# Router logits of the dilated heads: class-ordered read from SBUF, stepped write to PSUM

## The chip, the cores and the metric

The kernel runs on one core of one Trainium2 chip. The metric is the device time of one execution in microseconds; several executions are taken and their median is given. The profile that is read below is of one such execution, taken by the hardware profiler.

A core has TensorE (PE), which multiplies matrices, VectorE (DVE), ScalarE (ACT) and GpSimd (POOL) for everything else, and SyncE (SP), which issues most of the transfers. Data lies in SBUF, in 128 partitions. TensorE reads its two operands from SBUF and writes to PSUM, from where DVE or ACT fetch the result.

## The reference

Two blocks follow each other. The first is windowed attention over a batch of 8, with 8 heads, 576 positions and 64 features a head. The first four heads are plain: a position sees the 32 positions up to itself. The last four are dilated by 4: a position sees every fourth of the last 128. The second block is a mixture of 8 experts over the 4608 tokens with 512 features each (8 heads x 64):

```python
logits = np.einsum('bsd,de->bse', x, w_gate)
local_gate = 1.0 / (1.0 + np.exp(-np.einsum('bsd,de->bse', x, w_local).squeeze(-1)))
...
        fresh_e = int(np.argmax(logits[b, s]))
        if s == 0 or local_gate[b, s] < 0.5:
            e = fresh_e
        else:
            e = prev_e if prev_e >= 0 else fresh_e
...
        h = np.maximum(x[b, s] @ w1[e], 0.0)
        out[b, s] = p[e] * (h @ w2[e])
```

So each token has 8 logits and one locality value, and goes either to the expert with the largest logit or to the expert of the token before it. Everything is in float32. The change concerns the first two lines, the matrix product of the features with `w_gate` and `w_local`.

## The kernel before

**Stages.** The attention stage runs until some 158 us; then the experts' stage runs to the end. A second, exact version of the whole is in the program and runs only if a value leaves its bounds (`again > 0`, line 208); it does not run here.

**Order of a dilated head.** On the host, q, k and v of the dilated heads are put in the order of their class, that is of the position modulo 4 (`_by_class`, line 1231): first the 144 positions 0, 4, 8, ..., then 1, 5, 9, ..., and so on (`DIL` = 4, `CI` = 144, `S` = 576). In this order dilated attention is plain attention within a class. Its output stays in this order: in the tile `xt`, which holds the features of one pair of batches (`GB` = 2, `GS` = 1152 tokens) with features on the partitions, `xt[:, 0]` has the plain heads in natural order and `xt[:, 1]` the dilated heads in class order. Each has two chunks of 128 features (`CH` = 2), so there are `DK` = 4 chunks `kk` in all.

**Attention loop (line 1091).** Step `n` handles two heads of one batch. TensorE computes `scores(n)` (masks at L322 in bf16, scores at L329 in f32), ACT takes the exponential, and `values(n - 1)` multiplies with the values (L381), using `vt`, whose shifted part GpSimd copies (`share`, L270). Every second step `turn` transposes the finished heads into `xt` (L402, L406, copied by ACT at L403 and L408) and `store` writes them to DRAM. SyncE loads keys and values three steps ahead (L261, L266) into buffers that `values` frees.

**Routing.** When four pairs of heads of a pair of batches have been turned, `route` puts the routing steps of that pair into a list, `waiting`, and `gap` takes a few of them between the matmuls of the attention loop, by hand-written costs. The first step is `logits`, the next are `fresh` (transposes at L445), `carry` and so on, up to the lists of tokens of each expert. For the last pair of batches `logits` is called at once, at the end of the attention stage; its remaining steps run beside the first experts. Routing decides which rows GpSimd gathers (L847) and which weights SyncE loads (L773).

**`logits` (line 420).** `lp` is one PSUM bank of 128 partitions x 288 columns. The 1152 tokens are cut into `NC` = 4 runs of `NQ` = 288 tokens; run `c` goes to the 32 partitions from `c * LW`, each with its own column tile of the array (`tile_position=(0, c * LW)`), and the 9 used weight columns (padded to 32) are the stationary operand. For each chunk `kk` the four runs follow each other, and the four chunks accumulate in PSUM. For the plain heads (`kk` < 2) the moving operand is 288 neighbouring floats of each partition. For the dilated heads it has to be brought into natural order: element `4 j + c` is read from `xt[..., c * 144 + j]`. ACT then copies `lp` to `le` (L437), and `fresh` transposes `le`.

Of the kernel before, what the change touches and what calls it, by code (L numbers as in the profile page):

```python
# [23 lines left out]
B, H, S, DH = 8, 8, 576, 64  # L24
# [4 lines left out]
WIN, DIL = 32, 4  # L29
# [19 lines left out]
CH = 2  # L49
# [7 lines left out]
NQ = GS // NC  # L57
LW = 32
# [154 lines left out]
def whole(ctx, tc, exact, bad, qk, v, wgl, w1, w2, con, adm, msk, qmk, out, cst, wg, ones):  # L213
    nc = tc.nc
# [31 lines left out]
    def bank(shape, name):  # L246
        return banks.tile(shape, F32, name=name, tag="bank")
# [172 lines left out]
    def logits(g):  # L420

        st = routes[g]
        xt = st["xt"]
        lp = bank([P, NQ], "lp")
        for kk in range(DK):
            for c in range(NC):
                if kk < CH:
                    rhs = xt[:, 0, kk, c * NQ:(c + 1) * NQ]
                else:
                    b, s = divmod(c * NQ, S)  # L430
                    rhs = xt[:, 1, kk - CH, b * S:(b + 1) * S].rearrange("p (c j) -> p j c", c=DIL)
                    rhs = rhs[:, s // DIL:(s + NQ) // DIL]
                nc.tensor.matmul(lp[c * LW:(c + 1) * LW], lhsT=wg[:, kk], rhs=rhs,
                                 start=(kk == 0), stop=(kk == DK - 1), skip_group_check=True,
                                 tile_position=(0, c * LW))
        st["le"] = le = sm.tile([P, NQ], F32, name="le")
        nc.scalar.copy(le, lp)  # L437
# [613 lines left out]
    def route(g, slow):  # L1051
        steps = [(logits, 0, True), (fresh, 3.0, True), (carry, 1.0, True), (carry_over, 0.5, True), (carry_in, 0.5, True),
                 (choose, 1.5, True), (gate, 1.5, False), (place, 0.5, True), (lanes_of, 1.3, False)]
        if slow:
            logits(g)
            steps.pop(0)
        for f, *how in steps:
            waiting.append((lambda f=f: f(g), *how))
            if slow and f == fresh:
                waiting.append(pause)  # L1060
        waiting.extend((f, cost, False) for f, cost in zip(matrices(g), (0.9, 0.9, 0.9, 1.7)))
        if g in (EARLY - 1, NG - 1):
            late = g == NG - 1
            counts = count(late)
            steps = [(lambda: next(counts), 1.8, True)] * (PASSES + 1 if exact and late else 2)
            waiting.append(steps.pop())
            waiting.append((lambda: products(g, False), 0.3, True))
            waiting.extend(steps)
            waiting.append(pause)
            waiting.append((lambda: table(late), 0.3, True))  # L1070
            if late:
                waiting.append((late_tokens, 1.5, True))
            else:
                waiting.append((early_tokens, 1.5, True))
                waiting.append((early_weights, 0, False))
        else:
            waiting.append(pause)
            waiting.append((lambda: products(g, not g), 0.3, True))
# [200 lines left out]
```

## Time and profile before

| | |
|---|---|
| time, median of 3 runs | 675.02 us (674.6 to 676.7) |
| the profiled execution, whole | 672.8 us |
| its span, first to last instruction | 670.9 us |
| `logits` matmuls, L433 | 128 records, mean 544 ns |
| copy of `lp` by ACT, L437 | 4 of 398 ns |
| DMA moved | 126.38 MB, mean 188 GB/s |

A page of the profile gives the busy time of each engine, the span in forty equal slices (a digit is the busy share in tenths), and groups of equal instructions: line, engine, operation, output and inputs with their shape, count, then the time that the group covers, the mean of one in nanoseconds, and the idle time of the engine before it with what ended it. Other views list the instructions in order of time, the waits by who was waited for, or stretches of time with each engine's busy time (in brackets the number of instructions), TensorE's granted clock as a share of full speed, the share of time that the 16 DMA engines were busy, and GB/s. Records that run at the same time on different parts of TensorE's array count once in a group's covered time and each in full in its mean. An f32 matmul appears as two records.

### The profile page before, as it was taken

The numbers are of one execution on the slowest core, as the hardware profiler recorded it, in microseconds if no ns is written. First come the engines' busy times: TensorE is split into PE (matmuls) and PEld (weight loads), VectorE is DVE, ScalarE is ACT, GpSimd is POOL, SyncE is SP. The second block draws the span as 40 slices with busy tenths as digits, with TensorE's granted clock in tenths as the row PEclk, the third lists the DMA queues.
The fourth block names the chain that finished last, engine by engine and source line by source line (L and its number), as shares of the span: only waits on it lengthen the run. The fifth ranks groups of instructions, "written<-read, shape, count | busy, mean of one in ns | idle before, by whom it ended". The sixth has DMA issues, their size and how long they took to land. (4 is left out here: it accounts for less than half of the span.)

```text
span 670.9 us, 15284 instructions
## 1 busy us (share of the span) xinstructions
PE 655.1 (98%) x6466; PEld 572.1 (85%) x6466; DVE 373.7 (56%) x755; ACT 188.7 (28%) x348; POOL 186.6 (28%) x162
## 2 busy tenths in 40 slices
PE   8999999999999999999999999999999999999996
PEld 6988888787769999999589989997889988899893
DVE  3548669474397587363455581727373637446441
ACT  3544343432112232322223213222222232213210
POOL 3322212132023420321560343414044213041011
PEclk9999999999999999999999999999999999999999
DMA  8989889746403289666452545741054452353001
GB/s 325 321 274 310 279 263 324 244 138 240 196 33 146 91 355 386 228 221 214 140 233 75 219 173 185 288 143 60 9 189 166 182 218 98 123 221 145 1 33 49
DMA packets 29357, 126.38 MB, mean 188 GB/s; under 512 B 4221, under 2 KB 13789, under 8 KB 25312
## 3 DMA queue, kind: packets, MB, share of 16 engines
q1 hardware_dynamic: 22480, 106.10, 43.7%
q0 software_dynamic: 6800, 19.21, 8.3%
q8 instruction: 53, 0.87, 0.5%
q14 instruction: 24, 0.20, 0.1%
HBM read 142.07 MB, written 19.20 MB: 240 GB/s over the span
## 5 line engine op out<-in xcount | busy, mean ns | idle before, releaser
L971 POOL DMA_INDIRECT out_dram<-y,tok x36 | 55.0, 1528 | 297.0 <-DVE y L1040 124.0
L943 PE MATMUL hp<-xc,sum 128*128 128x128 f32 x720 | 85.6, 276 | 0.4 <-DVE sum L810 0.4
L943 PEld LDWEIGHTS hp<-xc,sum 128*128 128x128 f32 x720 | 82.8, 192 | 0.8 <-PE hp L943 0.5
L1025 PE MATMUL yp<-sum,hc 128*128 128x256 f32 x360 | 82.7, 380 | 0.0
L953 DVE TENSOR_TENSOR h<-hp,h 128x512 f32<-128x512 f32 x45 | 30.9, 690 | 90.4 <-PE hp L943 89.7
L1025 PEld LDWEIGHTS yp<-sum,hc 128*128 128x128 f32 x360 | 68.3, 190 | 9.6 <-ACT y L1033 0.4
L1040 DVE SCALAR_TENSOR_TENSOR y<-yp,gate,y 128x256 f32<-128x256 f32 x45 | 21.7, 482 | 75.3 <-issue 48.1
L270 POOL COPY vt<-vt 32x1040 f32<-32x1040 f32 x32 | 34.5, 1081 | 95.8 <-DMA vt<-in_v_dram 67.8
L943 PE MATMUL hp<-xe,raw 128*128 128x128 f32 x480 | 58.8, 276 | 0.0
L943 PEld LDWEIGHTS hp<-xe,raw 128*128 128x128 f32 x480 | 56.6, 192 | 1.8 <-issue 1.5
L1025 PE MATMUL yp<-raw,h 128*128 128x256 f32 x240 | 57.0, 381 | 0.0
L847 POOL DMA_INDIRECT xg<-xd,tok x40 | 46.0, 1149 | 38.1 <-PE hp L943 15.3
L329 PE MATMUL two<-kq 64*96 64x64 f32 x1152 | 54.9, 245 | 0.0
L329 PEld LDWEIGHTS two<-kq 64*96 64x96 f32 x1152 | 52.8, 162 | 0.0
L1025 PEld LDWEIGHTS yp<-raw,h 128*128 128x128 f32 x240 | 44.5, 190 | 5.5
L947 ACT COPY h<-hp 128x512 f32<-128x512 f32 x45 | 26.3, 585 | 79.3 <-PE hp L943 75.4
L334 DVE SCALAR_TENSOR_TENSOR pr<-two,mk 96x512 f32<-96x512 f32 x32 | 21.9, 684 | 47.9 <-ACT pr L336 37.7
L381 PE MATMUL pv<-vt,pr 96*64 96x65 f32 x1280 | 46.1, 226 | 2.1 <-POOL vt L270 1.6
L847 POOL DMA_INDIRECT xg<-xd,pos x40 | 44.2, 1104 | 12.1 <-issue 10.7
L954 ACT ACTIVATE h<-h 128x512 f32<-128x512 f32 x45 | 28.3, 630 | 67.2 <-DVE h L953 67.2
L381 PEld LDWEIGHTS pv<-vt,pr 96*64 96x64 f32 x1280 | 41.0, 139 | 5.1 <-POOL vt L270 1.9
L1033 ACT ACTIVATE y<-yp,gate 128x256 f32<-128x256 f32 x45 | 21.2, 473 | 56.1 <-PE yp L1025 50.0
(222 smaller groups left out, 1013.4 us busy)
## 6 DMA issues: line engine op xcount, KB each, us to landing
raw<-in_w_dram SPq DMA_DIRECT2D x48, 2048.0 KB
kq<-in_qk_dram SPq DMA_DIRECT2D x32, 592.0 KB
vt<-in_v_dram SPq DMA_DIRECT2D x32, 292.5 KB
xd<-x SPq DMA_DIRECT2D x16, 512.0 KB
raw<-in_w_dram SPq DMA_DIRECT2D x4, 512.0 KB
xd<-x SPq DMA_DIRECT2D x16, 64.0 KB
xg<-xd,tok POOLq DMA_INDIRECT x40, 3.2
xg<-xd,pos POOLq DMA_INDIRECT x40, 3.3
```

Source lines behind the costliest of these rows:

```text
L270: nc.gpsimd.tensor_copy(vt[:WIN, :, 1:], vt[QB:, :, :NB - 1])
L329: nc.tensor.matmul(sc[:KW, u, (i - a) * QB:(i - a + 1) * QB], lhsT=kt[h, i * QB:i * QB + KW], rhs=qt[h, i * QB:(i + 1) * QB], start=bool(a ...
L334: nc.vector.scalar_tensor_tensor(pr, sc[:KW, :, :w], -CEIL, mk[:, kind].unsqueeze(1).to_broadcast([KW, 2, w]), Alu.max, Alu.min)
L381: nc.tensor.matmul(pv[h * QB:(h + 1) * QB, k - a, u], lhsT=p[:, u, (i - c) * QB:(i - c + 1) * QB], rhs=vt[:, u, i], start=True, stop=True, ...
L847: nc.gpsimd.indirect_dma_start(out=x[:rows, g], out_offset=None, in_=xd[g] if units[u]["late"] else xd[g][:EARLY * GS], in_offset=bass.Ind ...
L943: nc.tensor.matmul(to[:, m], lhsT=a[:, m, kk], rhs=b[:, kk], start=first and m == 0 and kk == 0, stop=(kk == DK // 2 - 1), skip_group_chec ...
L947: nc.scalar.copy(at((0, 1, 3)[k]), of)
L953: nc.vector.tensor_tensor(at(k), of, at(k), op=Alu.add)
L954: nc.scalar.activation(at(k), at(k), Act.Relu)
L971: nc.gpsimd.indirect_dma_start(out=out, out_offset=bass.IndirectOffsetOnAxis(ap=of_unit(u, "tok", j), axis=0), in_=y, in_offset=None, boun ...
L1025: nc.tensor.matmul(to, lhsT=a[:, m], rhs=b[:, m], start=first and m == 0, stop=(m == FK // 2 - 1), skip_group_check=True)
L1040: nc.vector.scalar_tensor_tensor(at(k), of, of_unit(u, "gate", k // 2), at(k), Alu.mult, Alu.add)
```

## The change

Only the moving operand and the output of the dilated heads' matmuls in `logits` are described differently. Before, the operand was read in natural order: the inner index went over the 4 classes, 144 floats apart, the outer over 72 positions `j` one float apart. The output was 288 neighbouring columns. Now the inner index of the operand goes over 72 neighbouring positions, and the outer over the 4 classes. The output is given the same order: for each class 72 columns that are four columns (16 bytes) apart in PSUM. Each product still reaches the same column of `lp`. The plain heads' matmuls, the weights, the accumulation flags and the number of matmuls are as before.

```diff
             for c in range(NC):
+                to = lp[c * LW:(c + 1) * LW]
                 if kk < CH:
                     rhs = xt[:, 0, kk, c * NQ:(c + 1) * NQ]
                 else:
                     b, s = divmod(c * NQ, S)
-                    rhs = xt[:, 1, kk - CH, b * S:(b + 1) * S].rearrange("p (c j) -> p j c", c=DIL)
-                    rhs = rhs[:, s // DIL:(s + NQ) // DIL]
-                nc.tensor.matmul(lp[c * LW:(c + 1) * LW], lhsT=wg[:, kk], rhs=rhs,
+                    rhs = xt[:, 1, kk - CH, b * S:(b + 1) * S].rearrange("p (c j) -> p c j", c=DIL)
+                    rhs = rhs[:, :, s // DIL:(s + NQ) // DIL]
+                    to = to.rearrange("p (j c) -> p c j", c=DIL)
+                nc.tensor.matmul(to, lhsT=wg[:, kk], rhs=rhs,
                                  start=(kk == 0), stop=(kk == DK - 1), skip_group_check=True,
                                  tile_position=(0, c * LW))
```

## The prediction

> **What bounds the kernel now.** I read the page's busy times first, then its forty slices, then the groups of instructions kept apart by shape, then the timeline and the stretches around the touched matmuls, and last what TensorE waited for.
>
> ```profile
> PE 655.1 (98%) x6466; PEld 572.1 (85%) x6466; DVE 373.7 (56%) x755; ACT 188.7 (28%) x348; POOL 186.6 (28%) x162
> ...
> PE   8999999999999999999999999999999999999996
> ...
> L433 PE MATMUL lp<-xt,wg 128*32 128x288 f32 x128 | 12.7, 544 | 0.0
> ...
> L437 ACT COPY le<-lp 128x288 f32<-128x288 f32 x4 | 1.6, 398 | 10.5 <-PE lp L433 10.5
> ```
>
> TensorE is busy 655.1 of 670.9 us, in every slice, and no other engine passes 56%. So time taken from TensorE should come off the end, unless a stage is held by something else. The change touches one group, L433: 128 records that together cover 12.7 us. Four of them run beside each other, since each writes its own 32 rows of `lp`; hence 544 ns each and 12.7 us for all. There are four calls of `logits`, one per pair of batches, each with 4 chunks `kk` x 4 column tiles `c` x 2 records (the trace shows an f32 matmul as two records) = 32 records, that is 8 passes of four.
>
> The timeline around the first call, TensorE alone (start, us, engine, line, operation, count):
>
> ```profile
> 41.97 0.34 PE L406 MATMUL tp<-cst,x 64*128 64x64 f32 x2
> 42.24 3.20 PE L433 MATMUL lp<-xt,wg 128*32 128x288 f32 x32
> 45.36 0.41 PE L322 MATMUL two<-am 64*96 64x320 bf16 x6
> ```
>
> From the first start to the start of the next line 3.12 us pass. Asked in narrow windows, the same line gives the starts of the passes:
>
> ```profile
> L433 PE MATMUL lp<-xt,wg x4: 406/406/406, 42.7 to 42.8; 128*32 128x288 f32 x4
> ...
> L433 PE MATMUL lp<-xt,wg x4: 676/686/690, 44.2 to 44.2; 128*32 128x288 f32 x4
> ```
>
> Passes begin at 42.24, 42.49, 42.74, 42.99, then 43.24, 43.70, 44.22 and 44.74. The first four (kk 0 and 1, the plain heads, read as 288 neighbours) take 0.25 us each. The last four (kk 2 and 3, the dilated heads, each element 144 floats from the one before) take 0.46, 0.52, 0.52 and 0.62 us, the last with the drain until the next line starts; a record grows from 406 to some 680 ns. As two stretches:
>
> ```profile
> 42.24:43.24 1.00, 1.00 (x18) 0.55 (x21) 1.00 0.84 335
> 43.24:45.36 2.12, 2.12 (x20) 0.44 (x12) 1.00 0.81 235
> ```
>
> The granted clock is 1.00 in both, so the doubling is the access pattern's, not the throttle's. The other calls agree: 81.45 to 84.58, 129.14 to 132.26 and 157.82 to 160.92, thus 3.13, 3.12 and 3.10 us.
>
> Does anything else set the pace around these calls? The DMA engines are nearly full before 112 us (0.98 to 1.03 of their time in some 4 us stretches), so a faster TensorE could meet late loads. Its list of waits has the largest of that kind as
>
> ```profile
> PE hp L943 <- DVE h L953: 1.7, 2, 0.9
> PE pv L381 <- POOL vt L270: 1.6, 2, 1.2
> ```
>
> 1.6 us for the shifted value tile, both times in 136 to 160 us, and the score matmuls of L329 never waited for their keys. GpSimd waited 67.8 us for value loads at L270, but that reached TensorE only there: in the tightest place I looked at, the copy that starts at 63.85 ends at 64.89 and its reader starts at 67.77, 2.9 us later.
>
> [...]
>
> **The change, part by part.**
>
> *Removed:* the strided read in 4 of 8 passes of each call. The new read is four runs of 72 neighbours, three jumps in 288 elements. At the price of kk 0 and 1 those passes would take 4 x 0.25 = 1.00 us, plus the drain at the end of the call, which I take from the last pass: 0.62 - 0.50 = 0.12 us. So 2.12 becomes 1.12: 1.00 us saved a call, 4.0 us in all, if the write costs nothing.
>
> *Added:* PSUM writes 16 bytes apart in the same passes[...]. There is no row for it; I bound it. From below: nothing, a pass stays at 0.25 us. (Less than the contiguous pass is excluded, as the matmul and its operands are the same.) From the trace's fastest contiguous write, the bf16 mask matmuls of L322: two of them, on different rows of the array and into different banks, pass in the 0.18 us before the next line:
>
> ```profile
> 53.86 0.34 PE L322 MATMUL two<-am 64*96 64x320 bf16 x2
> 54.04 1.66 PE L329 MATMUL two<-kq 64*96 64x64 f32 x36
> ```
>
> 320 columns in 0.18 us is 0.56 ns a column[...]. The f32 pass delivers a column only every 0.25 us / 288 = 0.87 ns. [...] So f32, being slow itself, hides most or all of what would hurt bf16. From above: [...] I estimate four contiguous passes, 1.00 us. I take 0.25[...].
>
> *Unchanged:* 16 matmuls a call, their weights, flags and waits, no DMA, no queue moved. Each value lands in the same column of `lp`, so L437 (398 ns) and the transposes at L445 see the same layout. L437 starts earlier by what the call saves; its 10.5 us of waiting is ScalarE's and is in nobody's way.
>
> *Where the saving goes.* After calls one to three, scores of the next heads follow directly on TensorE (45.36, 84.58, 132.26), and after the fourth L917, the first expert. Loads are issued by SyncE when TensorE frees a buffer, so they move with it; the gathers hang on the routing that moves too. From 172 us on TensorE has no wait over 1 us, so the end moves with it. What could be late next is the value tile, with 2.9 us of slack at the tightest place seen, where 1.0 us has been gained; I charge nothing, and up to 1.0 us for the range. One more thing can move: from 149.2 to 152.6 us the granted clock is halved, after a stretch with only 1.98 us of TensorE work in 3.2:
>
> ```profile
> 146.00:149.20 3.20, 1.98 (x50) 1.77 (x48) 2.65 (x11) 1.33 (x2) 1.55 (x2) 1.00 0.58 193
> 149.20:152.60 3.40, 3.40 (x33) 2.83 (x27) 1.43 (x5) 0.92 (x2) 1.51 (x2) 0.50 0.14 39
> ```
>
> In it 8 transposes of L402 took 1.97 us against 1.09 elsewhere. Shifted work may meet this differently, by about 1 us either way.
>
> *Sum:* span 670.9 - 4.0 = 666.9; the profiled execution took 672.8, so it would take 668.8. The median of the runs shown is 675.02, 2.2 above that execution (674.6 to 676.7), so the forecast against it is 675.0 - 4.0 = 671.0 us.
>
> **The rivals.**
> - *Absorbed.* Passes drop to 0.25 us but late loads take most of it back before 160 us, where the loads end. Only the fourth call's 1.0 us is left for certain: 674.0. For it: DMA shares near 1.0. Against: no wait of L329, and slack in the value tiles. Chance 0.05.
> - *Trade of one stride for the other.* [...] 0.50 to 0.65 us. Four passes then take 2.0 to 2.6 us, plus 0.12, against 2.12: 0.0 to +0.6 us a call, 675.0 to 677.4. For it: the strided read shows that a fetch of one f32 alone does double a pass, although f32 is slow already; the f32 rate hid nothing there. [...] Chance 0.15, a fifth of it beyond 677.
> - *The write is worse than the read (the slower side).* Place: kk 2 and 3 of `logits`, in PSUM. [...] 1.00 us a pass: 4.12 against 2.12, +2.0 us a call, +8.0 in all, 683.0. It decides from 0.50 us a pass upward, and is measurable from 0.63 (2 us / 16 passes above 0.50). [...] Chance 0.32.
>
> **How the numbers follow.** The forecast, passes at 0.25 to 0.32 us, has 0.48. It spans 671.0 - 1.4 (an earlier end by the clock) to 671.0 + 4 x 4 x 0.07 + 0.7 = 672.8, so 669.6 to 672.8 for itself. A measurement of this kernel tells about 0.3% from no change, 2.0 us. Faster by more: the forecast, 0.48. Within: absorbed 0.05 and four fifths of the trade 0.12, so 0.17. Slower: 0.32 + 0.03 = 0.35. The range runs from 669.6 to 683.5 and leaves out some 0.05 below, and the costlier third of the last rival above, 0.11.
>
> **What would show it.** In the changed profile the group at L433 should have a mean near 410 ns instead of 544 and cover some 8.8 us instead of 12.7; a call should last about 2.1 us from its first start to the next line's. If kk 2 and 3 keep records of some 680 ns the trade is right; at 1,000 ns or more the slower rival. If L433 shrinks and the span doesn't, new waits at L381 or L329 for loads would show the absorption. The prediction is wrong if a pass with the stepped write takes more than 0.4 us.

## The result and the profile after

| | before | changed |
|---|---|---|
| time, median of 22 runs each | 676.66 us (674.6 to 681.13) | 673.79 us (669.37 to 679.94) |
| ratio to the kernel before | | 0.9948, 95% interval 0.9928 to 0.9967 |
| the profiled execution, whole | 672.8 us | 670.79 us |
| its span | 670.9 us | 668.9 us |

The ratio, which leaves out one slow run of the changed kernel, is 3.5 us less (2.2 to 4.9 us, taken of 676.66), where the two medians differ by 2.9. 4.0 us less was forecast. In the changed kernel the `logits` matmul stands at line 435 and the copy at 439. From the page's busy times, and from the groups kept apart by shape:

```profile
PE 649.8 (97%) x6466; PEld 571.0 (85%) x6466; DVE 373.1 (56%) x755; ACT 188.7 (28%) x348; POOL 185.3 (28%) x162
...
L435 PE MATMUL lp<-xt,wg 128*32 128x288 f32 x128 | 8.6, 409 | 0.1
L435 PEld LDWEIGHTS lp<-xt,wg 128*32 128x32 f32 x128 | 3.9, 109 | 3.0 <-PE tp L406 0.2
L439 ACT COPY le<-lp 128x288 f32<-128x288 f32 x4 | 1.6, 398 | 6.4 <-PE lp L435 6.4
```

The group covers 8.6 us in place of 12.7, and one record takes 409 ns in place of 544. ScalarE's copy is as long as before and waits 4.1 us less for it. The timeline of TensorE around the first call, and the same call cut at the fourth pass into two stretches:

```profile
42.35 2.15 PE L435 MATMUL lp<-xt,wg 128*32 128x288 f32 x32
44.43 0.41 PE L322 MATMUL two<-am 64*96 64x320 bf16 x6
```

```profile
42.35:43.35 1.00, 1.00 (x17) 0.55 (x21) 1.00 0.95 331
43.35:44.43 1.08, 1.08 (x20) 0.39 (x12) 1.00 0.97 355
```

The second half, which writes PSUM four columns apart, now takes 1.08 us, of which the drain is part; it took 2.12. A pass late in that half looks like the early ones:

```profile
L435 PE MATMUL lp<-xt,wg x4: 406/406/406, 44.1 to 44.1; 128*32 128x288 f32 x4
```

406 ns: the stepped write adds nothing to an f32 pass. All four calls last 2.08 us, so they give back 1.04, 1.05, 1.04 and 1.02 us, 4.15 together. The first expert's matmul, before and then changed:

```profile
160.92 2.43 PE L917 MATMUL hp<-xe,raw 128*128 128x256 f32 x10
```

```profile
156.73 3.72 PE L919 MATMUL hp<-xe,raw 128*128 128x256 f32 x16
```

It starts 4.19 us earlier, yet the span is only 2.0 us shorter: 2.2 us are lost again in the experts' stage, which the change doesn't touch. TensorE's longest waits in the changed kernel:

```profile
PE pv L381 <- POOL vt L270: 2.1, 4, 0.8
PE cold L283 <- DVE before L300: 1.9, 1, 1.9
PE hp L945 <- DVE h L955: 1.7, 2, 0.9
PE tp L406 <- DVE rec L385: 1.7, 2, 0.9
PE yp L987 <- issue: 1.5, 2, 1.1
PE hp L945 <- DVE sum L812: 1.0, 1, 1.0
```

Of these, longer than before are, in the attention stage, L381 by 0.5 us and L406 by 0.9; in the experts' stage L987, a stop of 1.5 us for which the profile shows no releaser, and L945's wait for DVE's weight sums, by 0.6 us. That the attention stage nevertheless gave the whole 4.15 us is in part accident: in the profile of before it holds the spell of half clock from 149.2 to 152.6 us (0.50), in that of the changed kernel none (1.00 in each stretch from 142 to 160 us).

So three questions were left: why the write costs nothing, whether all of the 4.15 us reaches the end, and whether the 2.2 us in the experts' stage is a price of the change.

### The profile page after: what moved, and what is told of

It is laid out like the page before. It is cut to its first block, busy times and chain, and to the rows that moved or that the text cites. A ratio compares the mean times of both kernels' runs of the same rounds, so it can differ in the third digit from the quotient of the medians.

```text
span 668.9 us, 15284 instructions
## 1 busy us (share of the span) xinstructions
PE 649.8 (97%) x6466; PEld 571.0 (85%) x6466; DVE 373.1 (56%) x755; ACT 188.7 (28%) x348; POOL 185.3 (28%) x162
## 5 line engine op out<-in xcount | busy, mean ns | idle before, releaser
L945 PE MATMUL hp<-xc,sum 128*128 128x128 f32 x720 | 85.7, 275 | 1.0 <-DVE sum L812 1.0
L945 PEld LDWEIGHTS hp<-xc,sum 128*128 128x128 f32 x720 | 82.9, 192 | 1.4 <-PE hp L945 1.1
L945 PE MATMUL hp<-xe,raw 128*128 128x128 f32 x480 | 58.8, 276 | 0.0
L945 PEld LDWEIGHTS hp<-xe,raw 128*128 128x128 f32 x480 | 56.6, 192 | 1.8 <-issue 1.5
L381 PE MATMUL pv<-vt,pr 96*64 96x65 f32 x1280 | 45.9, 224 | 2.3 <-POOL vt L270 2.1
L381 PEld LDWEIGHTS pv<-vt,pr 96*64 96x64 f32 x1280 | 40.8, 137 | 5.3 <-POOL vt L270 2.6
```

What stands on the lines that cost most here:

```text
L381: nc.tensor.matmul(pv[h * QB:(h + 1) * QB, k - a, u], lhsT=p[:, u, (i - c) * QB:(i - c + 1) * QB], rhs=vt[:, u, i], start=True, stop=True, ...
L945: nc.tensor.matmul(to[:, m], lhsT=a[:, m, kk], rhs=b[:, kk], start=first and m == 0 and kk == 0, stop=(kk == DK // 2 - 1), skip_group_chec ...
```

## The experiments

**A stepped write at bf16's rate.** The first question has two answers: the step is free, or f32 is too slow to show its cost. The bf16 mask matmuls can tell. The identity that they read has its columns permuted on the host, so the read stays in one run and the result is the same.

```diff
-    m = np.concatenate([np.eye(QB)] + [np.where(m, 0.0, MASK) for m in m], 1)
+    eye = np.eye(QB).reshape(QB, QB // 4, 4).transpose(0, 2, 1).reshape(QB, QB)
+    m = np.concatenate([eye] + [np.where(m, 0.0, MASK) for m in m], 1)
...
-                        nc.tensor.matmul(sc[:KW, u, rows[0] * QB:rows[1] * QB],
+                        to = sc[:KW, u, rows[0] * QB:rows[1] * QB]
+                        nc.tensor.matmul(to.rearrange("p (i j c) -> p i c j", j=QB // 4, c=4),
...
-                                         rhs=am[h, :QB].unsqueeze(1).to_broadcast([QB, rows[1] - rows[0], QB]),
+                                         rhs=am[h, :QB].rearrange("p (c j) -> p c j", c=4).unsqueeze(1).to_broadcast([QB, rows[1] - rows[0], 4, QB // 4]),
```

> The changed kernel, and besides it the bf16 mask matmuls (320 columns, two rows of tiles at once, 0.18 us a pair) write four columns apart in PSUM too, with the identity's columns permuted so that the result and the read stay the same. Theory A, the slow f32 rate hides the step: [...] a pair grows from 0.18 us to about 0.30 to 0.36 us and the attention stage by 32 x 0.12 to 0.18 = 4 to 6 us. Theory B, a step of four columns in PSUM costs a matmul nothing at any of these rates: a pair stays at 0.18 us and the time is the changed kernel's.

The group of the larger mask matmuls in the changed kernel, where they still write neighbouring columns; then the groups of this kernel, and one pair in its timeline:

```profile
L322 PE MATMUL two<-am 64*96 64x320 bf16 x64 | 11.4, 329 | 0.8 <-DVE pr L334 0.8
```

```profile
L324 PE MATMUL two<-am 64*96 64x320 bf16 x64 | 15.6, 463 | 0.8 <-DVE pr L336 0.8
...
L324 PE MATMUL two<-am 64*96 64x64 bf16 x64 | 5.3, 250 | 0.0
```

```profile
54.62 0.47 PE L324 MATMUL two<-am 64*96 64x320 bf16 x2
54.89 1.71 PE L331 MATMUL two<-kq 64*96 64x64 f32 x36
```

The group covers 15.6 us where it covered 11.4, and a pair takes 0.27 us from its start to the next line, where it took 0.18. So the step costs bf16 half as much again: 0.27 us / 320 = 0.84 ns for a lone column, against 0.56 for one of a contiguous run. Theory A holds in kind, a little below its lower figure (0.30 us). The small masks (64 columns), which add to what is in PSUM where the larger ones overwrite, pay too: 250 ns for one in place of 198. An f32 pass brings a column only every 0.87 ns (0.25 us / 288), so it can hide the step, but nothing is left over. In the trace's own start times the stepped f32 passes follow each other every 0.242 us (43.347, 43.589, 43.832 and 44.074), 0.84 ns a column, and the bf16 pair takes 0.27 us, also 0.84 ns: the two paces can't be told apart. One reservation stays: the masks run as two matmuls on different rows of the array into two banks, `logits` as four on different columns into one. That the pace alone makes the difference between bf16 and f32 fits both, but a bf16 matmul in the place of the f32 one wasn't run. The time of this kernel, 672.12 us in its one run beside 672.27 for the kernel before, tells little beside a scatter of several us; the rows above carry the reading.

**Other distances.** The same edit with steps of 2 and of 16 columns.

> The changed kernel, with the bf16 mask matmuls writing two columns (8 bytes) apart instead of four. The run with four columns showed a pair at 0.27 us against 0.18. [...]

> The changed kernel, with the bf16 mask matmuls writing sixteen columns (64 bytes) apart. If the cost is one access for each lone column, however far apart: 0.27 us a pair, as with four columns. If it grows with the distance: more than 0.30 us.

With a step of two columns, then with sixteen:

```profile
L324 PE MATMUL two<-am 64*96 64x320 bf16 x64 | 15.8, 469 | 0.8 <-DVE pr L336 0.8
```

```profile
L324 PE MATMUL two<-am 64*96 64x320 bf16 x64 | 15.6, 463 | 0.8 <-DVE pr L336 0.8
```

15.8 and 15.6 us: the cost comes in full at a step of 8 bytes and doesn't grow to 64. Pairs of neighbouring columns with gaps between the pairs weren't run, so what a pair costs isn't shown. The one time of each of these runs, 682.06 and 682.38 us, lies 10 us above that of the run with four columns, and 5 above the median of the kernel before beside them (677.39). The mask rows are alike and don't explain that. In both profiles TensorE waits 2.9 us for `xe` from ScalarE; the mean granted clock is 0.992 and 0.997.

**The same question for the read.** Before, the elements lay 576 bytes apart. Here the plain heads too are read with a step (and written with the same one, so that the result stays), of 16 bytes and of 8.

```diff
                 if kk < CH:
-                    rhs = xt[:, 0, kk, c * NQ:(c + 1) * NQ]
+                    rhs = xt[:, 0, kk, c * NQ:(c + 1) * NQ].rearrange("p (j c) -> p c j", c=4)
+                    to = to.rearrange("p (j c) -> p c j", c=4)
```

(`c=2` for the step of 8 bytes.)

> The changed kernel, and besides it the plain heads are read four floats (16 bytes) apart and written four columns apart; the result is the same. Theory A, [...] the four passes of kk 0 and 1 take 0.52 us instead of 0.25 and a call 2.08 + 1.08 = 3.2 us. Theory B, the doubling before came from the long hop of 576 bytes: passes stay at 0.25 to 0.3 us and a call at 2.1 us. If read step and write step added up, a pass would be longer than 0.52 us.

> The changed kernel, and besides it the plain heads are read two floats (8 bytes) apart and written two columns apart; the result is the same. [...] passes stay at 0.25 us and a call at 2.1 us. If any step on the read costs: passes of kk 0 and 1 between 0.3 and 0.5 us, a call at 2.3 to 3.1 us.

A pass of kk 0 (first) and one of kk 2 (second) with the 16-byte read, from narrow windows, then the timeline of the first call with the 16-byte and with the 8-byte read:

```profile
L436 PE MATMUL lp<-xt,wg x4: 688/690/692, 43.8 to 43.8; 128*32 128x288 f32 x4
...
L436 PE MATMUL lp<-xt,wg x4: 423/423/424, 45.3 to 45.3; 128*32 128x288 f32 x4
```

```profile
43.27 3.20 PE L436 MATMUL lp<-xt,wg 128*32 128x288 f32 x32
46.40 0.41 PE L322 MATMUL two<-am 64*96 64x320 bf16 x6
```

```profile
43.27 2.19 PE L436 MATMUL lp<-xt,wg 128*32 128x288 f32 x32
45.39 0.41 PE L322 MATMUL two<-am 64*96 64x320 bf16 x6
```

With 16 bytes a record takes 690 ns and a call 3.13 us, as long as the kernel before; with 8 bytes a call takes 2.12 us, 0.04 more than in the changed kernel. So a step of 16 bytes doubles a pass just as one of 576 does (0.52 us in place of 0.25), and one of 8 bytes doesn't: the long hop isn't what the read was charged for. The 16-byte run has both steps in kk 0 and 1, and its passes (43.3, 43.8, 44.3, 44.8, 45.3) are no longer than those with the read step alone. So the write step is free beside the slow read too. Whether two costs would add isn't tested by that, since an f32 pass pays nothing for the write step by itself.

**Does a saved us reach the end?** Both kernels with every call's matmuls done three times over, which makes three times the difference.

```diff
-        for kk in range(DK):
+        for kk in [*range(DK)] * 3:
```

> The kernel before, with the 16 matmuls of each logits call done three times over in the same bank (the first matmul of each turn overwrites; the result is the last turn's). Theory A, every us of these matmuls is a us of the end: 4 calls x 2 turns more x 3.0 us = +24 us against before, about 700 us. Theory B, the attention stage is held by loads, so calls one to three are partly covered: clearly under +24 us, down to +6 us if only the fourth call counts.

> The changed kernel, with the 16 matmuls of each logits call done three times over. Theory A: +4 x 2 x 2.0 = +16 us against the changed kernel, and 3 x 4.16 = 12.5 us under the kernel before with three turns. Theory B, loads hold the attention stage: the two kernels with three turns differ by much less than 12.5 us, 3 us if only the fourth call counts.

First call of the kernel before, then of the changed one, three turns each:

```profile
43.08 9.07 PE L433 MATMUL lp<-xt,wg 128*32 128x288 f32 x96
52.08 0.41 PE L322 MATMUL two<-am 64*96 64x320 bf16 x6
```

```profile
42.95 6.03 PE L435 MATMUL lp<-xt,wg 128*32 128x288 f32 x96
48.91 0.41 PE L322 MATMUL two<-am 64*96 64x320 bf16 x6
```

A call takes some 9.02 us and 5.96 us, so four calls differ by 12.2 us. The times are 1.0357 (1.0328 to 1.0385) and 1.0177 (1.0151 to 1.0203) of the kernel before; their difference of 0.0180 is 12.2 us of 676.67 (about 2.6 us either way, if the two intervals are independent). What TensorE saves here reaches the end whole, within that; an absorbed version, in which 3 us remain, is outside it. From before alone, 1.0357 is +24.2 us for 23.6 us more in the calls. But both kernels with three turns are slower than the kernel before, so loads have more time in them than in the changed kernel. What speaks against absorption in the changed kernel itself is its gain of 3.5 us: the interval, 2.2 to 4.9, excludes the 1.0 us that would be left, and of the waits that hang on loads only L381's grew, by 0.5 us.

**Is the loss in the experts' stage the change's?** Both kernels once more, for their profiles.

> The changed kernel once more, for its profile. Theory A, what the first profile lost in the experts' stage is chance: the stall of 1.5 us at the output of the half and few units and the later start at 221 us don't come back or come elsewhere, and the stage takes about 504 us as before. Theory B, the earlier end of the attention stage costs the experts' stage something: it takes about 506 us again, with the same waits.

> The kernel before once more, for its profile: an experts' stage of 504 us again if the first profile was typical; 505 to 507 us if the stage varies by chance from one execution to the next.

From the first expert's matmul to the start of TensorE's last one the changed kernel took 505.4 us and now 506.4, with the same waits, as theory B had said; but the kernel before took 503.4 us and now 506.7. TensorE's waits there, in the second profile of the kernel before:

```profile
PE hp L943 <- DVE sum L810: 1.6, 1, 1.6
PE yp L985 <- issue: 1.2, 3, 0.6
```

These are the same two waits that had looked like a price of the change, in a kernel without it. In three kernels that have the change (the bf16 write of four columns and the two reads) the stage took 503.1, 502.8 and 503.1 us; in the other profiles of this document it took 504.8 to 506.5 us with the change and 505.9 without (the kernel before with three turns). So both kernels spread over the same 3 to 4 us, and nothing in these profiles makes the 2.2 us a price of the change: the first profile of before was a short one, that of the changed kernel wasn't. Why the stage varies is open. The median of executions, not the pair of profiles, is the measure here.

The attention stage varies more, as these two profiles also show. The second one of the changed kernel took 681.23 us. Its stretches from 136 to 144 us:

```profile
136.00:140.20 4.20, 2.40 (x53) 2.03 (x50) 3.28 (x8) 1.42 (x3) 2.01 (x2) 0.99 0.67 214
140.20:144.00 3.80, 3.80 (x35) 3.26 (x33) 1.14 (x5) 1.34 (x3) 2.01 (x2) 0.50 0.12 35
```

After 4.2 us in which TensorE worked only 2.40, its granted clock is halved (0.50), and stays so in every stretch up to 164.0 us. The attention stage without its `logits` calls (the first expert's start, 166.3 us, less four calls of 2.08) takes 158.0 us there and 148.4 in the first profile. How much of the 9.6 us is the clock's, and how much belongs to waits that came with it, isn't separated.

**Two attempts on that scatter.** The first puts routing work behind the transposes, so that VectorE is free when TensorE wants `rec` and `x` from it; the second gives TensorE unused work in three places where it idles.

```diff
-        gap(SHARE)
+        turns = n >= 3 and n % 2 == 1
+        if not turns:
+            gap(SHARE)
...
+        if turns:
+            gap(SHARE)
         gap(SHARE)
```

```diff
+        if not exact and m in (6, 13, 14):
+            nc.tensor.matmul(bank([P, 512], "cold"), lhsT=warm[:, :P], rhs=warm, start=True, stop=True)
         tp = bank([P, CH, S - full], "tp")
```

> The changed kernel; in the steps with a transpose of finished heads the routing work put between the matmuls comes behind the transpose instead of ahead of the values. Theory A, the scatter and the rest of the missing gain come from VectorE's routing work holding up the transposes (2.2 and 2.4 us at L406 near 70 us in two profiles), after which the granted clock is halved for 7 to 24 us: with VectorE free at the transposes there are fewer such spells and the median falls by 1 to 3 us below the changed kernel's. Theory B, the waits only move to the routing's own small matmuls: the same time as the changed kernel or up to 3 us more.

> The changed kernel, with one unused f32 matmul of 512 columns (about 0.9 us) ahead of the last transposes of three of the sixteen transposes, those near 71, 138 and 146 us, where TensorE idles. Theory A, idleness of TensorE brings the spells of half clock: they become rarer and the median falls by 0 to 2 us, with less scatter. Theory B, idleness isn't their cause: up to 2.6 us more than the changed kernel, with the same spells.

The reordered kernel took 1.0010 (0.9988 to 1.0032) of the time of before, so it loses what the change gained, some 4 us (about 2 either way). That is against theory A; theory B had up to 3 us. In the profiled execution TensorE waits for the routing, as theory B said:

```profile
PE two L329 <- DVE gates L532: 2.5, 1, 2.5
```

The mean granted clock of this execution is 0.949. But it took 705.25 us where the median is 678.55, so it doesn't explain the others, and the cause of the loss is open. The filled kernel took 0.9978 (0.9958 to 0.9998), no better than the changed kernel's 0.9948. In its profile the idle time was in another place:

```profile
152.00:155.70 3.70, 1.45 (x24) 1.15 (x18) 2.45 (x10) 0.19 (x1) 2.07 (x2) 0.98 0.30 85
155.70:162.50 6.80, 6.36 (x43) 3.29 (x43) 3.79 (x5) 2.22 (x5) 0.00 (x0) 0.51 0.84 274
```

TensorE waited 2.7 us for `xe` from ScalarE, at a place that wasn't filled, and the half clock followed (0.51). The same wait, of 2.9 us, stands in the unfilled kernels with steps of 2 and 16 columns, so the fill needn't have brought it. The time fits theory B; but as the spell came where nothing was filled, the run doesn't refute theory A, nor does it show that idleness brings the spells. Neither version is better than the changed kernel. What decides the length of such a spell wasn't found.

## Why the prediction was right

- *The removed cost.* Forecast: 2.12 us of a call become 1.12, 1.00 saved, 4.0 in all. Measured: 1.08, 1.04 saved, 4.15 in all by the trace and 3.5 (2.2 to 4.9) by the times. The 0.04 us is the drain, which took 0.08 us where 0.12 was put (0.62 less the 0.52 us of the strided passes, in place of 0.50, would have been 0.10). The forecast of 671.0 us stood on a median of 675.02 from 3 runs; with 22 it is 676.66, which makes 672.7 of it, beside 673.79 measured.
- *The added cost.* Forecast: nothing, or at most 0.07 us a pass. The upper figure was the author's estimate: it allowed a lone column twice the 0.56 ns of one in the contiguous bf16 masks, a factor that no trace showed, and so 0.32 us for a pass of 0.25. Measured: nothing for f32 (0.25 us a pass), and a lone column costs 0.84 ns in bf16. The argument held, that f32's own pace of 0.87 ns covers the step. That nothing at all is added is in part luck: the estimate left up to 0.07 us a pass open, and the two paces turned out equal as far as they can be read (0.84 ns each), so f32 has nothing to spare.
- *The rival of the trade* (0.50 to 0.65 us a pass) and *the slower one* (1.00 us) fall with a pass of 0.25 us. Both figures were the author's estimates, and for the slower one, with its chance of 0.32, no trace spoke. What spoke for the trade, that the strided read was not hidden by f32, was true but didn't carry over: a lone element costs about 0.52 us / 288 = 1.8 ns to read and 0.84 ns to write.
- *The absorption*, which leaves 1.0 us, falls with the gain of 3.5 us (2.2 to 4.9); the runs of three turns agree, 12.2 us by the times and 12.2 by the calls.
- *The rest.* The 1 us charged to the clock was too little for a single execution: with half clock from 140.2 to 164.0 us (0.50) the attention stage was 9.6 us longer. Such spells occur in both kernels; how much they move the medians' difference was not tested by itself.

## What to carry to other kernels

When an f32 matmul must reorder its columns, put the step on the PSUM side and read SBUF in runs: here the stepped write added nothing to an f32 pass (0.25 us), the read in steps of 16 or 576 bytes doubled it (0.52 us). With bf16 the same write cost half as much again (0.27 us for a pair of masks against 0.18), so weigh it there. Before blaming a change for time lost in a stage it doesn't touch, profile the kernel before a second time.

## What the hardware showed beyond that

In three profiles half clock (0.50 or 0.51) followed a stretch in which TensorE idled: in the kernel before it was busy for 1.98 of 3.2 us (146.0 to 149.2), in the second profile of the changed kernel for 2.40 of 4.2 (136.0 to 140.2), and in the filled kernel for 1.45 of 3.7 (152.0 to 155.7). Steady work didn't end a spell at once: in the second profile of the changed kernel TensorE was busy through all 15.8 us from 140.2 to 156.0, and its granted clock stayed at 0.50. What begins and ends such a spell isn't shown.
